# An attention and two-MLP kernel on one core: whole tiles of 64-bit words, eight heads a group, copies of q and v on GpSimd, plain products with the last weights

## The chip, the cores and the metric

One core of a Trainium2 chip runs the whole kernel as one launch. The metric is the device time of that launch in microseconds. TensorE (PE) multiplies, VectorE (DVE), ScalarE (ACT) and GpSimd (POOL) do the elementwise work, and all transfers of the kernel are issued from SyncE's queue (SP). Each engine takes its instructions in the order in which the program put them; an instruction that waits holds up everything behind it on its engine.

## The reference, cut to what matters

```python
def _attn_ref(q, k, v, g_q, g_k):            # 4 batches, 12 heads, 448 tokens, head size 64
    def rmsnorm(x, g):
        return x / np.sqrt(np.mean(x * x, axis=-1, keepdims=True) + 1e-06) * g
    q_n, k_n = rmsnorm(q, g_q), rmsnorm(k, g_k)
    scores = (1 / np.sqrt(64)) * np.matmul(q_n, k_n.transpose(0, 1, 3, 2))
    attn = np.exp(scores - np.max(scores, axis=-1, keepdims=True))
    attn = attn / (np.sum(attn, axis=-1, keepdims=True) + 1e-09)
    return np.matmul(attn, v)
# heads side by side: x is 1792 x 768
h = x @ w_in;  x = np.maximum(0.01 * h, h) @ w_out             # 768 -> 2048 -> 768
out = (((x @ w1) * (x @ w2)) @ w3) @ w_last                     # 768 -> 1024 -> 1024 -> 768
```

q, k and v are float32. The five weight matrices are float64, and the kernel gets them as pairs of 32-bit words.

## The kernel before, in words

**Arithmetic.** A product of float32 matrices is made of three float32r products: each operand is split into a high and a low part (a copy to float32r on ScalarE, then a subtraction of the copy from the operand), and TensorE multiplies high by high, high by low and low by high. The helper `copy` (L100 to L106) is a copy on ScalarE ("A"), VectorE ("V") or GpSimd ("P"), and `subtract` (L190 to L192) is the subtraction, on GpSimd or VectorE; so all of them stand in the profile at L102, L106 and L192, and are told apart by their tiles.

**Attention.** There are 48 heads and 50 steps. In step s, `attention_steps` (L392) emits the values of head s-2, the four transposes of the softmax of head s-1, the four score tiles of head s, and then the preparations: `keys(s+5)`, `load_v(s)`, `v_split(s)`, `prep(s+2)`, `load(s+3)` and `statistics(s+6)`. A score tile goes from TensorE (L272, L273) to VectorE, which scales it and takes the extreme of each row (L276), to ScalarE for the exponential (L285). Its transposes (L316) go to ScalarE (the high part, tile pth) and then VectorE (the low part, tile ptl), and then TensorE multiplies them with v (L370). `prep` splits q: the copy qh on ScalarE, the subtraction ql on GpSimd. `v_split` splits v of heads 8 to 47 in the same way.

`statistics(i)` (L127) does nothing but for the heads i that begin a group in `GROUPS` (L38): two heads at 0 and at 2, then four heads at 4, 8 and so on to 44. For a group it loads q and k of each head, squares them on ScalarE (L140) and sums them on VectorE (L141); then VectorE makes 1 / rms of all of the group's heads at once, by a shift and three Newton steps on a tile of 112x32 (`inverse_root`, L114 to L125; group 0 takes a power on GpSimd instead). The part for k is written to DRAM and read back spread over the partitions in `keys` (rk_sb, L238), for two heads at a time; there VectorE multiplies k by it (L239).

**MLP work between the steps.** The weights' own product w3 @ w_last is made first (`combine_weights`, tile wc), and then the two MLPs for batches 0 and 1. `fill` (L1024) spreads their matmuls between the attention steps in proportion to the steps done. After every third matmul `group` (L523) calls `pump`, which emits one more piece of weight preparation as long as fewer than two prepared tiles are waiting (`AHEAD`).

**64-bit words.** `Weights.work` (L494) prepares a weight tile of 128x768 or 128x512 in four pieces: `split`, `to_float32` for each half, and `load`. `to_float32` (L450) works on half a tile, 384 or 256 words, with five operations: ScalarE scales the high words (L467), GpSimd keeps the sign (L468), VectorE shifts and merges (L469), ScalarE scales the low words (L472), and GpSimd adds them (L473). 80 tiles come as 64-bit words: 8 of w_last, 16 of w_in and 16 of w1 and w2 (768 words wide), 16 of w3 and 24 of w_out (512 words wide). Each is loaded in two halves.

**Last pair of batches.** When the attention is done, the MLPs of batches 2 and 3 run alone (L1077 on). The products with w_in, w1 and w2 are made from 2x2 blocks with seven products instead of eight (`quads`, L852; `Operands.put`, L801, makes the sums of the operand, `Blocks`, L700, those of the weights). The products with w_out are plain (`group`, L918). The products with wc, the last of the kernel, are made from blocks as well: `of_hidden` (L831) has tiles for seven operands, `h.put` (L939, L943) fills them, and `quads(ONE, ...)` (L962) multiplies; this happens twice, for g = 0 and 1. The low parts of the weights of the second MLP are subtracted on GpSimd (`eng`, L747), those of the first on VectorE.

**Order.** A scheduler that plays a timeline through when the program is built sets the order on each engine from readiness and priority: `PRIORITY` (L43) ranks the attention functions, and weight preparation has 100.

Of the kernel before, what the change touches and what calls it, by code (L numbers as in the profile page):

```python
# [8 lines left out]
F32 = mybir.dt.float32  # L9
# [11 lines left out]
P = 128  # L21
# [16 lines left out]
GROUPS = {0: 2, 2: 2, **{i: 4 for i in range(4, 48, 4)}}  # L38
MAX_GROUP = 4
# [9 lines left out]
def attention_then_moe(  # L49
# [22 lines left out]

# [14 lines left out]
    cv = right(name="cv", bufs=4)  # L87
# [38 lines left out]

    def statistics(i):  # L127

        n = GROUPS.get(i)
        if n is None:  # L130
            return
        m = NCH * n
        ss = small.tile([CP, 2, MAX_GROUP * NCH], F32, tag="ss", name="ss", bufs=2)[:, :, :m]
        for j in range(n):
            b, e = divmod(i + j, H)
            x = io.tile([CP, 2, NCH, D], F32, tag="qk", name="qk_sb", bufs=2)
            nc.sync.dma_start(x, qk[b, e])
            after = exps.get(i - STATS_AHEAD)
            with tc.issue_after(after.ins) if after else ExitStack():
                nc.scalar.activation(x, x, AF.Square)  # L140
            nc.vector.tensor_reduce(  # L141
                ss[:, :, j * NCH : (j + 1) * NCH], x, axis=AX.X, op=ALU.add
            )
# [107 lines left out]
    def v_split(i):  # L251
# [4 lines left out]
        copy("A", h["vs"][:, :, 0], h["v"])  # L256
# [157 lines left out]
    class Weights:  # L414
# [20 lines left out]
        def load(self, t):  # L435
# [6 lines left out]
            self.words[t] = []  # L442
            for e in range(2):
                x = cv.tile([P, WT // 2, 2], U32, tag="w64", name="w64")
                half = src[:, e * n : (e + 1) * n].rearrange("p (n t) -> p n t", t=2)
                with tc.issue_after(start["ins"].ins) if t < 2 else ExitStack():
                    nc.sync.dma_start(x[:, : n // 2], half)
                self.words[t].append(x)

        def to_float32(self, t, e):  # L450
# [8 lines left out]
            m = self.size(t) // 2  # L459
            if e == 0:  # L460
                self.raw[t] = wp.tile([P, WT], F32, tag="raw", name="raw")
            words = self.words[t][e]
            low, high = words[:, :m, 0], words[:, :m, 1]
            out = self.raw[t][:, e * m : (e + 1) * m]
# [3 lines left out]
            nc.gpsimd.tensor_scalar(signed, signed, 0.0, 1.0, op0=ALU.mult, op1=ALU.mult)  # L468
            nc.vector.scalar_tensor_tensor(  # L469
# [3 lines left out]
            nc.gpsimd.tensor_tensor(top, top, low, op=ALU.add)  # L473

        def split(self, t):
# [3 lines left out]
            self.words.pop(t, None)  # L479
# [14 lines left out]
        def work(self):  # L494
            n = len(self.sources)
            for t in range(-2, n):
# [3 lines left out]
                if 0 <= t + 1 < n and self.sources[t + 1][1]:  # L500
                    for e in range(2):
                        self.to_float32(t + 1, e)
                        yield
# [196 lines left out]
    class Blocks:  # L700
# [5 lines left out]
        def __init__(self, sources, shared):  # L706
            self.sources, self.shared = sources, shared
# [27 lines left out]
        def work(self):  # L735
            self.load(0)
            yield
            for q, of in enumerate(self.sources):
# [8 lines left out]
                eng = "P" if q >= self.shared else "V"  # L747
# [5 lines left out]
                self.split(a, ("wh", "wl"), wp, eng)  # L753
# [10 lines left out]
                self.split(f[1], ("wh", "wl"), wp, eng)  # L764
# [26 lines left out]
    class Operands:  # L791
# [9 lines left out]
        def put(self, k, what, x):  # L801
# [3 lines left out]
            if what != "12":  # L805
                two(x, t[{"11": 1, "21": 2, "22": 3}[what]], k, "V")
            sub = nc.vector.tensor_tensor
            if "t2" not in f and all(n in f for n in ("11", "12", "22")):
                f["t1"], f["t3"], f["t2"] = f["11"], f["12"], f["22"]
# [5 lines left out]
                two(f["t1"], t[5], k, "V")  # L815
            if "t4" not in f and "t2" in f and "21" in f:
# [14 lines left out]
    def of_hidden():  # L831
        return Operands(
            {
                p: [
                    [
                        last["pool"].tile([P, S], F32R, tag=f"g{part}", name=f"g{part}", bufs=14)
                        for _ in range(KG // 2)
                    ]
                    for part in "hl"
                ]  # L840
                for p in range(1, 8)
            }
        )

    ONE = [(0, x) for x in "b1 c7 b6 a2 b5 c4 b3".split()]
    TWO = [
# [5 lines left out]
    def quads(order, qs, xs, use):  # L852

        banks = {}
        for i, (bank, p) in order:
# [28 lines left out]
    def first_of_last():  # L884

        q = 0
        for g in range(NG):
# [3 lines left out]
            def use(i, p, ps):  # L891
# [6 lines left out]
                else:  # L898
                    return
                x = tuple(  # L900
                    last["pool"].tile([P, S], F32R, tag=f"g{part}", name=f"g{part}", bufs=14)
                    for part in "hl"
                )
                copy("A", x[0], y[i, what])
                subtract("V", x[1], y[i, what], x[0])
                gs[int(what[1]) + 1][2 * i + int(what[0]) - 1] = x

            yield from quads(TWO, [q, q + 1], last["x"], use)
            q += 2
            if g == NG - 1:  # L910
                last["x2"] = of_features()
            for m in range(NO):
                w = blocks.weights(q)
                w = [[x[:, k // 2, k % 2] for k in range(KG)] for x in w]
                q += 1
                for b in (3, 2):
                    ps = last["ps"].tile([P, 512], F32, tag="st", name="ps_o")
                    yield from group(blocks, ps, S, w, [gs[b][k] for k in range(KG)])  # L918
                    if g == 0:
                        acc_last(m, b)  # L920
                        nc.scalar.activation(acc[m, b], ps[:, :S], AF.Copy)
                    else:
                        nc.vector.tensor_tensor(acc[m, b], ps[:, :S], acc[m, b], op=ALU.add)
                    if g == NG - 1:
                        last["x2"].put(m // 2, f"{m % 2 + 1}{b - 1}", acc[m, b])
        last["q"] = q

    def second_of_last():
        q, x = last["q"], last["x2"]
        for g in range(2):  # L930
            h = of_hidden()
            for k in range(KH2 // 2):
                y = {}

                def use(i, p, ps):
                    if partial(y, i, p, ps) and p == 4:
                        a = y[i, "11"]
                        nc.vector.tensor_tensor(a, a, y[i, "21"], op=ALU.mult)
                        h.put(k, "21" if i else "11", a)  # L939
                    elif p == 3:  # L940
                        b = y[i, "22"]
                        nc.vector.tensor_tensor(b, ps, b, op=ALU.mult)  # L942
                        h.put(k, "22" if i else "12", b)  # L943

                yield from quads(TWO, [q, q + 1], x, use)
                q += 2
            for n in range(NO // 2):

                def use(_, p, ps):
                    what = SUMS[p]  # L950
                    m, b = 2 * n + int(what[0]) - 1, int(what[1]) + 1
                    if p in (1, 7, 6, 3) and g == 0:
                        acc_last(m, b)
                        nc.scalar.activation(acc[m, b], ps, AF.Copy)
                    else:
                        nc.vector.tensor_tensor(acc[m, b], ps, acc[m, b], op=ALU.add)  # L956
                    if p in (2, 5, 4, 3) and g == 1:
                        nc.sync.dma_start(
                            out_t[m * P : (m + 1) * P, b * S : (b + 1) * S], acc[m, b]
                        )  # L960

                yield from quads(ONE, [q], h, use)  # L962
                q += 1

    def last_sources():
# [6 lines left out]
        for g in range(2):  # L972
            yield from pairs(kept[second_mlp, g])
            js = slice(g * KH2, (g + 1) * KH2)
            yield from pairs([wc[m, :, js].rearrange("p k c -> p (k c)") for m in range(NO)])

    def begin_last_pair():
# [11 lines left out]
        for k in range(KD // 2):  # L989
            for what in ("11", "12", "22", "21"):  # L990
                x = last["f"].tile([P, S], F32, tag="x_f", name="x_f", bufs=4)
# [59 lines left out]
    with tc.tile_pool(name="comb", bufs=1) as pool:  # L1051
# [16 lines left out]
        blocks = Blocks(list(last_sources()), NG * (KG // 2 + NO))  # L1068
# [8 lines left out]
    for part in first_of_last, second_of_last:  # L1077
        for _ in part():
            pass
# [44 lines left out]
```

## Time and profile before

| | |
|---|---|
| median of 3 runs | 1304.16 us (1303.16 to 1304.36) |
| the profiled execution | 1303.81 us |
| its span, first to last instruction | 1302.0 us |
| busy: PE, DVE, ACT, POOL | 1182.5, 847.3, 762.2, 643.2 us |
| mean granted TensorE clock | 0.959 |

The span is what the trace shows; the profiled execution's own time has 1.8 us more, that lie around it. Busy time is the sum of the engine's instructions, and the end of a matmul is modelled, so a busy TensorE may still be slowed. An idle time in brackets names what ended it.

### The profile page before, as it was taken

To read this page: it belongs to the slowest core of one execution; us is meant where nothing else is said; L and a number is where in the kernel's file an instruction comes from. 1 tells how busy PE (TensorE), PEld (TensorE's weight loads), DVE (VectorE), ACT (ScalarE), POOL (GpSimd) and SP (SyncE) were. 2 spreads that over 40 slices of the span, in tenths; PEclk is the share of its full clock that TensorE was granted. 3 is DMA by queue.
4 is the path that set the end of the run, shared out by engine and by line. 5 is a ranking of instruction groups with operands and counts; after the bars stand their busy time and mean duration, and the time that the engine had idled before them with its cause. 6 is when DMAs were issued, how large, how long until landed. Compare 5 with 4: busy or idle time off the path is not lost. (4 is left out here: it accounts for less than half of the span.)

```text
span 1302.0 us, 18289 instructions
## 1 busy us (share of the span) xinstructions
PE 1182.5 (91%) x5780; PEld 1015.7 (78%) x5780; DVE 847.3 (65%) x1593; ACT 762.2 (59%) x1657; POOL 643.2 (49%) x657
## 2 busy tenths in 40 slices
PE   3888989988888889999888999999999999899997
PEld 2436877877777779887777898898999999697986
DVE  6777676787967586773684444448346464986576
ACT  6676777787956667665674566535443434444432
POOL 6887666888933368776787447520000000222321
PEclk9889998998989899999999999999999999998999
DMA  8677666677674456574355245125112120211212
GB/s 240 166 177 212 180 165 190 197 201 193 191 200 146 126 151 181 166 206 140 115 167 183 85 115 175 55 92 191 54 45 81 33 82 25 84 46 46 72 46 85
DMA packets 108577, 172.66 MB, mean 133 GB/s; under 512 B 23776, under 2 KB 62656, under 8 KB 108480
## 3 DMA queue, kind: packets, MB, share of 16 engines
q1 hardware_dynamic: 108480, 171.50, 45.8%
q8 instruction: 45, 0.74, 0.2%
q14 instruction: 52, 0.43, 0.1%
HBM read 130.45 MB, written 30.45 MB: 124 GB/s over the span
## 5 line engine op out<-in xcount | busy, mean ns | idle before, releaser
L192 POOL TENSOR_TENSOR wl<-raw,wh 128x512 fp32r<-128x512 f32 (+1 forms) x97 | 156.1, 1609 | 321.7 <-ACT wh L730 252.8
L473 POOL TENSOR_TENSOR raw<-raw,w 128x384 uint32<-128x384 uint32 (+1 forms) x160 | 155.9, 981 | 39.2 <-DVE raw L469 31.1
L285 ACT ACTIVATE p<-p,low 112x448 f32<-112x448 f32 x192 | 126.9, 662 | 71.4 <-DVE p L276 71.0
L469 DVE SCALAR_TENSOR_TENSOR raw<-raw,w 128x384 uint32<-128x384 uint32 (+1 forms) x160 | 126.3, 803 | 60.0 <-POOL w L468 56.1
L316 PE MATMUL pt<-ident,p 112*112 112x112 f32 x768 | 119.2, 278 | 48.5 <-DVE ptl L192 33.9
L316 PEld LDWEIGHTS pt<-ident,p 112*112 112x112 f32 x768 | 89.2, 141 | 88.9 <-DVE ptl L192 39.1
L276 DVE TENSOR_SCALAR_CACHE_REDUCE p<-ps,rs 112x448 f32<-112x448 f32 x192 | 125.1, 676 | 40.7 <-PE ps L273 24.1
L192 DVE TENSOR_TENSOR ptl<-pt,pth 112x448 fp32r<-112x448 f32 x160 | 97.0, 616 | 79.3 <-ACT pth L102 77.9
L531 PE MATMUL ps_mm<-xh,wl 128*128 128x448 f32 x384 | 143.6, 375 | 1.2 <-POOL wl L192 1.2
L531 PE MATMUL ps_mm<-xh,wh 128*128 128x448 f32 x384 | 143.7, 375 | 0.8 <-ACT wh L489 0.8
L531 PE MATMUL ps_mm<-xl,wh 128*128 128x448 f32 x384 | 143.2, 373 | 0.0
L472 ACT ACTIVATE w<-w 128x384 uint32<-128x384 uint32 (+1 forms) x160 | 78.4, 491 | 96.5 <-DMA w<-w 41.2
L531 PE MATMUL ps_mm<-gh,wl 128*128 128x448 f32 x288 | 106.8, 374 | 1.2 <-DVE wl L192 1.0
L272 PE MATMUL ps<-ks,qh 128*112 128x448 f32 x192 | 79.9, 419 | 30.9 <-DVE p L276 22.4
L531 PE MATMUL ps_mm<-gl,wh 128*128 128x448 f32 x288 | 107.8, 376 | 0.0
L531 PE MATMUL ps_mm<-gh,wh 128*128 128x448 f32 x288 | 107.4, 377 | 0.2
L468 POOL TENSOR_SCALAR w<-w 128x384 f32<-128x384 f32 (+1 forms) x160 | 82.4, 527 | 39.6 <-ACT raw L467 34.5
L102 ACT ACTIVATE pth<-pt 112x448 fp32r<-112x448 f32 (+1 forms) x176 | 92.1, 532 | 16.0 <-PE pt L316 12.2
L467 ACT ACTIVATE raw<-w 128x384 f32<-128x384 f32 (+1 forms) x160 | 74.0, 487 | 39.9 <-DMA w<-w3t 9.4
L489 ACT ACTIVATE wh<-raw 128x512 fp32r<-128x512 f32 (+1 forms) x104 | 73.1, 704 | 17.4 <-PE ps_mm L531 13.0
L531 PEld LDWEIGHTS ps_mm<-xh,wh 128*128 128x128 f32 x384 | 73.7, 192 | 7.7 <-ACT wh L489 1.4
L531 PEld LDWEIGHTS ps_mm<-xh,wl 128*128 128x128 f32 x384 | 73.6, 192 | 7.6 <-POOL wl L192 1.4
(172 smaller groups left out, 3115.6 us busy)
## 6 DMA issues: line engine op xcount, KB each, us to landing
w<-w_in SPq DMA_DIRECT2D x32, 384.0 KB, 4.8
w<-w_out SPq DMA_DIRECT2D x48, 256.0 KB, 3.6
w<-w SPq DMA_DIRECT2D x32, 384.0 KB, 4.5
qk_sb<-qk SPq DMA_DIRECT2D x48, 224.0 KB, 4.0
qt_sb<-qt SPq DMA_DIRECT2D x96, 112.0 KB, 3.3
raw<-kept_first_mlp SPq DMA_DIRECT2D x24, 384.0 KB, 3.8
raw<-kept_first_mlp SPq DMA_DIRECT2D x36, 256.0 KB, 2.7
w<-w3t SPq DMA_DIRECT2D x32, 256.0 KB, 3.7
```

Source lines behind the costliest of these rows:

```text
L102: nc.scalar.activation(out, x, AF.Copy)
L192: e.tensor_tensor(out, x, y.bitcast(F32), op=ALU.subtract)
L272: nc.tensor.matmul(ps, h["qh"][:, q], h["ks"], start=True, stop=False)
L276: nc.vector.tensor_scalar(p, ps, h["scale"][:, c : c + 1], None, op0=ALU.mult, op1=ALU.min, accum_out=low,)
L285: exps[i] = nc.scalar.activation(p, p, AF.Exp, bias=low, scale=-1.0, accum_out=h["sum"][:, c : c + 1])
L316: nc.tensor.transpose(pt[:, c * CP : (c + 1) * CP], h["p"][c][:, kc * CP : (kc + 1) * CP], ident[:CP, :CP],)
L467: nc.scalar.activation(out, signed, AF.Copy, scale=2.0**-112)
L468: nc.gpsimd.tensor_scalar(signed, signed, 0.0, 1.0, op0=ALU.mult, op1=ALU.mult)
L469: nc.vector.scalar_tensor_tensor(top, top, 3, high, op0=ALU.logical_shift_left, op1=ALU.bitwise_or)
L472: nc.scalar.activation(low, low, AF.Copy, scale=2.0**-29)
L473: nc.gpsimd.tensor_tensor(top, top, low, op=ALU.add)
L531: nc.tensor.matmul(ps[:, :n], a, x, start=begin, stop=end, skip_group_check=on)
```

## The change

- `GROUPS` has eight heads a group from head 8 on. The squares and sums of a group's heads are emitted one head a step (`squares`), the last of them in the step that makes 1 / rms.
- The copies of q in `prep` and of v in `v_split` go from ScalarE to GpSimd.
- `to_float32` works on a whole tile, so each of its operations is emitted once a tile; the add of the low words goes from GpSimd to VectorE; its five operations are three pieces for `pump`. A tile is loaded at once, into one of two buffers of twice the size.
- Products with wc are plain: `quads(ONE, ...)` and `of_hidden` go, and `output_last`, which has the loops that the products with w_out had, serves both MLPs. Blocks remain for w_in, w1 and w2.
- The low parts of all block weights are subtracted on VectorE. In `Operands.put` the split of "22" comes after those of the sums, and t2 has a tile of its own.

```diff
-GROUPS = {0: 2, 2: 2, **{i: 4 for i in range(4, 48, 4)}}
+GROUPS = {0: 2, 2: 2, 4: 4, **{i: 8 for i in range(8, 48, 8)}}
...
+    def squares(i, h):
+        first = max(g for g in GROUPS if g <= h)
...
+        nc.sync.dma_start(x, qk[b, e])
...
+            nc.scalar.activation(x, x, AF.Square)
+        nc.vector.tensor_reduce(
+            sums[first][:, :, j * NCH : (j + 1) * NCH], x, axis=AX.X, op=ALU.add
+        )
...
     def statistics(i):
+        for g, m in GROUPS.items():
+            for j in range(m):
+                if i == (g if g < 8 else max(STATS_AHEAD, g - m + 1 + j)):
+                    squares(i, g + j)
         n = GROUPS.get(i)
...
-        copy("A", h["qh"], h["qt"])
+        copy("P", h["qh"], h["qt"])
...
-        copy("A", h["vs"][:, :, 0], h["v"])
+        copy("P", h["vs"][:, :, 0], h["v"])
...
-        def to_float32(self, t, e):
+        def to_float32(self, t):
...
             nc.scalar.activation(out, signed, AF.Copy, scale=2.0**-112)
             nc.gpsimd.tensor_scalar(signed, signed, 0.0, 1.0, op0=ALU.mult, op1=ALU.mult)
+            yield
             nc.vector.scalar_tensor_tensor(
                 top, top, 3, high, op0=ALU.logical_shift_left, op1=ALU.bitwise_or
             )
             nc.scalar.activation(low, low, AF.Copy, scale=2.0**-29)
-            nc.gpsimd.tensor_tensor(top, top, low, op=ALU.add)
+            yield
+            nc.vector.tensor_tensor(top, top, low, op=ALU.add)
+            yield
...
-                self.split(a, ("wh", "wl"), wp, eng)
+                self.split(a, ("wh", "wl"), wp, "V")
...
-                self.split(f[1], ("wh", "wl"), wp, eng)
+                self.split(f[1], ("wh", "wl"), wp, "V")
...
+    def output_last(q, gs, begin, done):
+        for m in range(NO):
+            w = blocks.weights(q + m)
+            w = [[x[:, k // 2, k % 2] for k in range(KG)] for x in w]
+            for b in (3, 2):
+                ps = last["ps"].tile([P, 512], F32, tag="st", name="ps_o")
+                yield from group(blocks, ps, S, w, [gs[b][k] for k in range(KG)])
...
-            h = of_hidden()
-            for k in range(KH2 // 2):
+            gs = {b: {} for b in (2, 3)}
+            for k in range(0, KH2, 2):
...
-                        h.put(k, "21" if i else "11", a)
+                        hidden_last(a, gs, 2, k + i)
...
-                yield from quads(ONE, [q], h, use)
...
+            yield from output_last(q, gs, g == 0, store if g else None)
```

`hidden_last` makes one high and one low part of a hidden tile: a copy on ScalarE and a subtraction on VectorE.

## Rows read from the trace of the kernel before

**Rows 1.** Stages (us): length, busy PE, PEld, DVE, ACT, POOL (count), PEclk, DMA.
```profile
20.00:850.00 830.00, 744.56 (x3698) 621.88 (x3697) 553.13 (x1102) 563.56 (x1309) 572.32 (x606) 0.94 0.58 164
850.00:1106.00 256.00, 254.53 (x1244) 232.82 (x1243) 137.74 (x226) 107.97 (x192) 9.41 (x7) 1.00 0.25 75
1106.00:1182.00 76.00, 70.19 (x330) 62.04 (x329) 66.81 (x109) 34.60 (x60) 20.69 (x9) 0.98 0.19 60
1182.00:1195.00 13.00, 10.51 (x34) 7.71 (x33) 9.24 (x15) 6.43 (x12) 2.54 (x2) 0.74 0.11 32
1195.00:1268.00 73.00, 73.00 (x356) 66.51 (x355) 47.99 (x81) 31.23 (x54) 20.52 (x12) 1.00 0.20 63
1268.00:1277.00 9.00, 6.06 (x20) 4.06 (x20) 6.97 (x11) 3.99 (x8) 1.36 (x2) 0.81 0.00 0
```

**Rows 2.** TensorE's waits, 20 to 850 us: total us, times, longest us.
```profile
PE pt L316 <- DVE ptl L192: 33.9, 25, 5.0
PE ps L272 <- DVE p L276: 22.4, 18, 4.6
```

**Rows 3.** Timeline of TensorE at two places: start, duration, idle time before.
```profile
434.74 0.71 PE L272 MATMUL ps<-ks,qh 128*112 128x448 f32 x1 [4.64 <-DVE p L276]
...
487.40 0.99 PE L316 MATMUL pt<-ident,p 112*112 112x112 f32 x4 [4.56 <-DVE ptl L192]
```

**Rows 4.** Timeline of VectorE at three places.
```profile
432.52 0.69 DVE L239 SCALAR_TENSOR_TENSOR kt_sb<-kt_sb,gqk,rk_sb 128x448 f32<-128x448 f32 x1 [7.92 <-DMA rk_sb<-rk]
...
482.81 1.74 DVE L123 SCALAR_TENSOR_TENSOR rt<-ss,rs 112x32 f32<-112x32 f32 x1
...
654.78 4.33 DVE L469 SCALAR_TENSOR_TENSOR raw<-raw,w 128x384 uint32<-128x384 uint32 x1
```

**Rows 5.** Timeline of GpSimd at the third of these places.
```profile
654.67 1.84 POOL L192 TENSOR_TENSOR wl<-raw,wh 128x768 fp32r<-128x768 f32 x1
656.48 2.23 POOL L192 TENSOR_TENSOR xl<-acc,xh 128x448 fp32r<-128x448 f32 x2
```

**Rows 6.** Sums of stages: 18 us from nine inverse roots; the stretches between.
```profile
sum 162.00, PE 128.98 PEld 107.66 DVE 114.94 ACT 95.18 POOL 99.62; mean PE 14.33 PEld 11.96 DVE 12.77 ACT 10.58 POOL 11.07
...
sum 486.00, PE 447.95 PEld 391.75 DVE 324.58 ACT 341.94 POOL 343.04; mean PE 49.77 PEld 43.53 DVE 36.06 ACT 37.99 POOL 38.12
```

**Rows 7.** Lines by form, VectorE, 20 to 850 us (mean ns).
```profile
L469 DVE SCALAR_TENSOR_TENSOR raw<-raw,w 128x384 uint32<-128x384 uint32 x78 | 64.1, 837 | 30.2 <-POOL w L468 26.4 <-DMA w<-w 3.7
L469 DVE SCALAR_TENSOR_TENSOR raw<-raw,w 128x256 uint32<-128x256 uint32 x80 | 60.4, 767 | 28.7 <-POOL w L468 28.5
...
L239 DVE SCALAR_TENSOR_TENSOR kt_sb<-kt_sb,gqk,rk_sb 128x448 f32<-128x448 f32 x23 | 25.3, 1101 | 57.6 <-DMA rk_sb<-rk 31.1 <-DMA kt_sb<-kt 9.0 <-issue 8.8
...
L116 DVE TENSOR_SCALAR rs<-ss 112x32 uint32<-112x32 uint32 x11 | 17.3, 1576 | 0.1
...
L192 DVE TENSOR_TENSOR wl<-raw,wh 128x512 fp32r<-128x512 f32 x12 | 14.6, 1224 | 7.4 <-ACT wh L489 7.4
...
L192 DVE TENSOR_TENSOR wl<-raw,wh 128x768 fp32r<-128x768 f32 x5 | 4.8, 952 | 1.2 <-ACT wh L489 1.2
```

**Rows 8.** Stage, VectorE, instructions on tile rt (L123 to L125).
```profile
20.00:850.00 830.00, 36.70 (x99) 0.94 0.58 164
```

**Rows 9.** The page's costliest groups: the adds of the low bits.
```profile
L473 POOL TENSOR_TENSOR raw<-raw,w 128x384 uint32<-128x384 uint32 (+1 forms) x160 | 155.9, 981 | 39.2 <-DVE raw L469 31.1
```

**Rows 10.** Lines by form, whole span, ScalarE and GpSimd.
```profile
L467 ACT ACTIVATE raw<-w 128x384 f32<-128x384 f32 x80 | 41.2, 547 | 19.4 <-DMA w<-w_last 8.3 <-DMA w<-w_in 6.0 <-POOL wl L192 4.7
...
L467 ACT ACTIVATE raw<-w 128x256 f32<-128x256 f32 x80 | 32.8, 427 | 20.5 <-DMA w<-w3t 9.4 <-DMA w<-w_out 8.5 <-POOL wl L192 1.6
...
L102 ACT ACTIVATE qh<-qt_sb 128x448 fp32r<-128x448 f32 x48 | 27.3, 568 | 1.7 <-DMA qt_sb<-qt 1.0 <-PE ps L272 0.6
...
L102 ACT ACTIVATE vs<-v_sb 112x256 fp32r<-112x256 f32 x40 | 16.4, 411 | 0.4
...
L106 POOL TENSOR_SCALAR kh<-kt_sb 128x448 fp32r<-128x448 f32 x23 | 14.6, 637 | 33.1 <-DVE kt_sb L239 33.1
```

More of the change, by code (lines that the diff above doesn't have):

```diff
@@ L125, in inverse_root @@
             nc.vector.scalar_tensor_tensor(r, t, 1.5, r, op0=ALU.add, op1=ALU.mult)
+    sums = {}
+    def squares(i, h):
+        first = max(g for g in GROUPS if g <= h)
+        if first not in sums:
+            sums[first] = small.tile([CP, 2, MAX_GROUP * NCH], F32, tag="ss", name="ss", bufs=2)
+        j = h - first
+        b, e = divmod(h, H)
+        x = io.tile([CP, 2, NCH, D], F32, tag="qk", name="qk_sb", bufs=2)
+        nc.sync.dma_start(x, qk[b, e])
+        after = exps.get(i - STATS_AHEAD)
+        with tc.issue_after(after.ins) if after else ExitStack():
+            nc.scalar.activation(x, x, AF.Square)
+        nc.vector.tensor_reduce(
+            sums[first][:, :, j * NCH : (j + 1) * NCH], x, axis=AX.X, op=ALU.add
+        )
     def statistics(i):
+        for g, m in GROUPS.items():
+            for j in range(m):
+                if i == (g if g < 8 else max(STATS_AHEAD, g - m + 1 + j)):
+                    squares(i, g + j)
         n = GROUPS.get(i)
@@ L132, in statistics @@
         m = NCH * n
[L133 to L143, printed above, removed]
+        ss = sums.pop(i)[:, :, :m]
         nc.vector.tensor_scalar(ss, ss, 1.0 / D, 1e-6, op0=ALU.mult, op1=ALU.add)
@@ L441, in load @@
                 return
[L442 to L448, printed above, removed]
-        def to_float32(self, t, e):
[L459 to L462, printed above, removed]
+            x = self.words[t] = cv.tile([P, WT, 2], U32, tag="w64", name="w64")
+            with tc.issue_after(start["ins"].ins) if t < 2 else ExitStack():
+                nc.sync.dma_start(x[:, :n], src.rearrange("p (n t) -> p n t", t=2))
+        def to_float32(self, t):
+            m = self.size(t)
+            self.raw[t] = wp.tile([P, WT], F32, tag="raw", name="raw")
+            words = self.words.pop(t)
             low, high = words[:, :m, 0], words[:, :m, 1]
-            out = self.raw[t][:, e * m : (e + 1) * m]
+            out = self.raw[t][:, :m]
             top = out.bitcast(U32)
@@ L500, in work @@
                 if 0 <= t + 1 < n and self.sources[t + 1][1]:
-                    for e in range(2):
-                        self.to_float32(t + 1, e)
-                        yield
+                    yield from self.to_float32(t + 1)
                 if t + 2 < n:
@@ L804, in put @@
             f[what] = x
-            if what != "12":
-                two(x, t[{"11": 1, "21": 2, "22": 3}[what]], k, "V")
+            if what in ("11", "21"):
+                two(x, t[{"11": 1, "21": 2}[what]], k, "V")
             sub = nc.vector.tensor_tensor
             if "t2" not in f and all(n in f for n in ("11", "12", "22")):
-                f["t1"], f["t3"], f["t2"] = f["11"], f["12"], f["22"]
+                f["t1"], f["t3"] = f["11"], f["12"]
+                f["t2"] = last["f"].tile([P, S], F32, tag="x_f", name="t2", bufs=5)
                 sub(f["t1"], f["12"], f["11"], op=ALU.subtract)
@@ L829, in of_features @@
         return Operands(tiles)
[L831 to L846, printed above, removed]
+    ORDER = [
         (int(x[0]), x[1:])
@@ L882, in acc_last, with hidden_last, last_pair @@
         acc[m, b] = last["f"].tile([P, S], F32, tag=name, name="acc", bufs=1)
-    def first_of_last():
+    def hidden_last(x, gs, b, k):
+        gs[b][k] = tuple(
+            last["pool"].tile([P, S], F32R, tag=f"g{part}", name=f"g{part}", bufs=8)
+            for part in "hl"
+        )
+        copy("A", gs[b][k][0], x)
+        subtract("V", gs[b][k][1], x, gs[b][k][0])
+    def output_last(q, gs, begin, done):
[5 more added lines that the diff above has]
+                yield from group(blocks, ps, S, w, [gs[b][k] for k in range(KG)])
+                if begin:
+                    acc_last(m, b)
+                    nc.scalar.activation(acc[m, b], ps[:, :S], AF.Copy)
+                else:
+                    nc.vector.tensor_tensor(acc[m, b], ps[:, :S], acc[m, b], op=ALU.add)
+                if done:
+                    done(m, b, acc[m, b])
+    def last_pair():
         q = 0
+        x2 = None
         for g in range(NG):
@@ L899, in use, with done @@
                     return
[L900 to L908, printed above, removed]
+                hidden_last(y[i, what], gs, int(what[1]) + 1, 2 * i + int(what[0]) - 1)
+            yield from quads([q, q + 1], last["x"], use)
             q += 2
+            done = None
             if g == NG - 1:
[L911 to L929, printed above, removed]
+                x2 = of_features()
+                def done(m, b, x):
+                    x2.put(m // 2, f"{m % 2 + 1}{b - 1}", x)
+            yield from output_last(q, gs, g == 0, done)
+            q += NO
         for g in range(2):
-            h = of_hidden()
-            for k in range(KH2 // 2):
+            gs = {b: {} for b in (2, 3)}
+            for k in range(0, KH2, 2):
                 y = {}
@@ L942, in use, with store @@
                         nc.vector.tensor_tensor(b, ps, b, op=ALU.mult)
-                        h.put(k, "22" if i else "12", b)
-                yield from quads(TWO, [q, q + 1], x, use)
+                        hidden_last(b, gs, 3, k + i)
+                yield from quads([q, q + 1], x2, use)
                 q += 2
[L947 to L960, printed above, removed]
-                yield from quads(ONE, [q], h, use)
-                q += 1
+            def store(m, b, x):
+                nc.sync.dma_start(out_t[m * P : (m + 1) * P, b * S : (b + 1) * S], x)
+            yield from output_last(q, gs, g == 0, store if g else None)
+            q += NO
     def last_sources():
@@ L974, in last_sources @@
             js = slice(g * KH2, (g + 1) * KH2)
-            yield from pairs([wc[m, :, js].rearrange("p k c -> p (k c)") for m in range(NO)])
+            yield from ([wc[m, :, js].rearrange("p k c -> p (k c)")] for m in range(NO))
     def begin_last_pair():
```

24 lines of the change are left out of this document (11 added, 13 removed).

## The prediction, made before the change was run

> **What bounds the kernel now.** I read the busy time by stage first [rows 1]. From 850 us on, in the last pair of batches, TensorE is the bound: 254.5 of 256 us busy at full clock in the first stretch, and in 1195 to 1268 us 356 matmuls take 73 us, which is 0.205 us each. Two holes break this, at 1182 and 1268 us. Before 850 us no engine is full: TensorE 745 of 830 us, VectorE 553, ScalarE 564, GpSimd 572. TensorE stands for 85 us there, and its mean granted clock is 0.94. Of its two levels, 1.2 and 2.4 GHz, that mean means 12% of the time at the lower, so some 50 us of work lost on top. This stage is a ring of queues in order, and the question is which wait ends last.
>
> The second view, TensorE's waits in that stage, says that: it waits for VectorE, 33.9 us for the low part of the transposed softmax (psum is freed by that subtraction) and 22.4 us for the scaled scores [rows 2]. Third, I went to the longest of these waits in the timeline. TensorE stood 4.64 us until 434.74 and 4.56 us until 487.40 [rows 3]. In the first, VectorE had been idle 7.92 us: the multiplication of k waited for 1 / rms to come back from DRAM, with the scores behind it in the queue. In the second, it was in the small operations of `inverse_root`, one of which took 1.74 us for 32 elements a partition [rows 4]. Both are events of a group of four heads. A third place is of another kind: one merge of 64-bit words took 4.33 us [rows 4] where the mean is 0.84 [rows 7], while GpSimd ran three subtractions without a gap [rows 5].
>
> To see what the group events weigh altogether I summed nine stretches of 18 us, each from the start of an inverse root, and the nine stretches between them [rows 6]. TensorE is busy 129.0 of 162 us (79.6%) in the first and 448.0 of 486 (92.2%) in the others. The 12.6% are 20.4 us, 2.3 us a group.
>
> **The change, part by part.**
>
> *Groups of eight.* From 13 groups it comes to 8: the five that began at 12, 20, 28, 36 and 44 go. At 2.3 us each that is 11.5 us. The five groups of eight have one head's loads, squares and sum in their step instead of four; so 1 / rms is ready earlier and the first keys of a group wait less. L239 stands idle 57.6 us in all [rows 7]. I take half of 2.3 us for each of these five, 6 us, between 0 (the trip to DRAM remains) and 11.5. The squares themselves are moved, not saved: six heads' loads, squares and sums now come in step 0, hidden by nothing, for the start is full; I leave that at up to 3 us, in the range. Sum: -17.5 us, between -8 and -23. The five roots also free VectorE: L116 at 1.576 us [rows 7], and 36.70 us of Newton steps over 11 groups, 3.34 us each [rows 8]; 4.9 us a group, 25 us in all, though they are counted within the 2.3 us already where TensorE felt them.
>
> *Whole tiles.* The 160 half-tile passes become 80.
> - ScalarE: 547 ns for 384 words against 427 for 256 [rows 10] leaves 187 ns that don't depend on the length; 160 fewer operations save 30 us.
> - VectorE's merge: 837 and 767 ns for 384 and 256 words [rows 7], 70 ns per 128 words. For 768 that gives 1.05 us, for 512 0.91, so 40 of each cost 78 us instead of 125: -46 us; at worst nothing is saved.
> - VectorE's new add: the trace has none. Its nearest rows are VectorE's subtractions from two SBUF tiles in this stage, 0.952 us for 768 and 1.224 for 512 columns [rows 7]; 40 of each are 87 us. Against uncontended work it could be some 70, and if each waits as long as the merges do it is 100.
> - GpSimd loses 155.9 us of adds [rows 9].
>
> *Copies of q and v.* ScalarE gives up 27.3 + 16.4 us. GpSimd's copy of k, 637 ns for 448 columns, is the nearest row [rows 10]: 48 of them are 31 us, and the 40 of v, with 256 columns, at most 25. GpSimd's own subtraction behind each copy no longer waits for ScalarE.
>
> Together in this stage: ScalarE -74 us of 564, GpSimd -100 of 572, VectorE +87 - 46 - 25 = +16 of 553. Only VectorE is what TensorE waits for. Sixteen us more of it, 3%, would cost TensorE between 0 (they fall where it waits anyway) and 16 us (each in front of a score). Against that, VectorE waited 55 us for GpSimd at the merges (the two idle times of L469 [rows 7]), behind a GpSimd that now has less to do and sends its part one `pump` earlier; if half of this goes and TensorE felt a third, that is 9 us. I take the two as equal: 0, between -25 and +25. In it are also the pieces of `pump`, five a tile instead of four, where a product with w_out for one batch gives only four chances, and the first operation of a tile that now waits for the whole load. Two prepared tiles in hand, and a freer ScalarE, hide both; without that cover it is the +25.
>
> A rule speaks against this part. Here one merge was held 4.33 us while three GpSimd operations passed [rows 4, 5]. The Trainium skill, "SBUF — State Buffer", section "Who interferes with whom", says that a VectorE instruction with two SBUF inputs contends with a GpSimd instruction that reads SBUF, and that the one which comes first keeps the shared port for its whole length. By that rule all 80 adds join the 80 merges in that contest, while GpSimd's own adds leave it; the trace agrees on who waits, but here the wait was longer than any one of the three instructions. What that could cost is the slower rival below.
>
> *The last pair.* Plain products with wc are 2 x 144 matmuls where blocks took 2 x 126: 36 more, 7.4 us at 0.205. What goes are the holes: the first output of each g needed sums of sums of the last hidden tile, and TensorE did 34 matmuls (7.0 us) in 13 us and 20 (4.1 us) in 9 [rows 1]: 6.0 + 4.9 = 10.9 us lost. In the plain form the last hidden tile needs one copy and one subtraction, and the matmuls that don't need it (the other three hidden tiles, and for the second batch twelve more) go first, 9 to 21 matmuls or 1.8 to 4.3 us of cover. Without that cover the holes stay and it is +7.4. VectorE takes 16 low parts of weights from GpSimd, 15 us at 0.952 [rows 7], which would matter around 1106 to 1182 us, where it is busy 66.8 of 76 us [rows 1]; but 28 operations for sums and parts of hidden tiles leave it, though none of them before 1130 us, so I allow +3 there. Sum: -3.5 us, between -7 and +10.
>
> **Sum**: 1303.8 (the profiled execution's own time; span 1302.0) - 17.5 + 0 - 3.5 = 1282.8. The median of the runs is 0.35 us above that execution: 1283.2.
>
> **Rivals.**
> - *More falls than the groups.* If VectorE, with shorter waits for both other engines, is late half as often everywhere, half of its 56.3 us [rows 2] goes, and with it the clock's loss in proportion (50 us lost per 85 us of standing): 28 x 1.6 = 45 us, then -3.5: 1255. For it: ScalarE and GpSimd fall by 13 and 17%. Against: VectorE's own load does not fall.
> - *VectorE held by GpSimd.* The slower one. GpSimd's copy and subtraction of q now run without a gap, as the three at 654.67 us did [rows 5], and every merge and add behind such a run waits. If the 160 VectorE operations wait 0.6 us more each, that is 96 us, and with the 16 above VectorE's load goes from 67 to 80%. A third of this in front of TensorE is +37, less 17.5 and 3.5: 1320. It decides from about 0.35 us more a wait (56 + 16 us, a third of which, 24, eats the 21). For it: the 4.33 us; that 512 columns took 1.224 us and 768 only 0.952 [rows 7], so waits of that order are there. Against: GpSimd is busy 69% now and 57% then.
> - *Given back.* The groups' 17.5 us are eaten by VectorE's 16 and its order: 1304 less 3.5, within about 1300 to 1306.
> - *The groups don't do it.* The round trip stays as late in each group that is left and only the five that go count, with squares crowded at the start: 1303.8 - 11.5 + 3 - 3.5 = 1292.
>
> **How the numbers follow.** Forecast (1265 to 1298) 0.48, more falls 0.15, groups don't do it 0.07, given back 0.10, VectorE held 0.20. About 0.2%, 2.6 us, is what a measurement of this kernel tells from no change. Faster takes the first three, with 0.02 of "given back": 0.72, less 0.02 for the forecast's own tail; "given back" leaves 0.07 within and a little above. So 0.70, 0.07, 0.23. The range leaves out half of the two outer cases: 1250 to 1315.
>
> **What would show it.** In the profile after: seven inverse roots instead of twelve, and TensorE's busy share after them near 90%; idle time of L239 about 20 us instead of 57.6; VectorE's merge near 1.0 us and its add below 1.2; TensorE's waits for VectorE about 40 us and a mean clock of 0.95 or more before 850 us; the last pair starting some 15 to 20 us earlier; no hole of several us in front of the products with wc. The prediction is wrong if merges or adds average over 1.4 us, if TensorE waits for weights, or if VectorE's waits for ScalarE's high part take the place of those removed.

## The result, and the profile after

The changed kernel takes 1286.5 us (median of 4 runs, 1284.3 to 1293.6) against 1304.1 before: a ratio of 0.9888, 95% interval 0.9857 to 0.9919. Measured again beside the variants below, on another chip on which the kernel before takes 1297.7, the ratio is 0.9918 (0.9892 to 0.9944). So the change is worth 1.0%, some 11 to 18 us; 1283.2 was forecast. The profiled execution took 1287.95 us, with a span of 1286.2.

The view of the stages, for the changed kernel, with the columns of [rows 1]:

```profile
20.00:852.00 832.00, 749.18 (x3764) 631.86 (x3765) 571.85 (x1044) 519.76 (x1073) 492.17 (x460) 0.96 0.56 165
...
1140.00:1286.00 146.00, 141.84 (x691) 129.25 (x689) 71.19 (x116) 46.05 (x80) 0.00 (x0) 1.00 0.19 63
```

The first row is to be held against the first of [rows 1]: in about the same time TensorE does 66 matmuls more (3764 to 3698). GpSimd is 80 us less busy, ScalarE 44 us less and VectorE 19 us more, where the sum had -100, -74 and +16 (busy time counts instructions that overlap at their ends once, and durations were summed). TensorE still stands for 83 us. The load of x for the last pair is issued at 852.3 us instead of 865.3, and from there to the end it is 433.9 us instead of 436.7.

TensorE's waits in that stage, as in [rows 2]:

```profile
PE pt L327 <- DVE ptl L203: 25.8, 17, 5.3
PE ps L283 <- DVE p L287: 16.4, 12, 4.5
PE pt L327 <- ACT pth L101: 4.3, 2, 2.5
```

The two waits for VectorE fall from 56.3 to 42.2 us. But over all rows of the view the sum falls only from 84.2 to 82.6: waits for ScalarE and GpSimd come up in their place (17.9 to 29.1 us). The rest of the stage's gain is in TensorE's busy time: the mean granted clock is 0.96 instead of 0.94. A second profile of the changed kernel has 0.95 there, so how much of that the change brings can't be told from it.

VectorE by line and form, 20 to 838 us, against [rows 7]:

```profile
L476 DVE SCALAR_TENSOR_TENSOR raw<-raw,w 128x768 uint32<-128x768 uint32 x39 | 49.1, 1262 | 37.1 <-POOL w L474 37.1
L481 DVE CUSTOM_DVE_ANT_0 raw<-w,raw 128x1536 uint16<-128x1536 uint16 x39 | 45.6, 1169 | 0.6
L476 DVE SCALAR_TENSOR_TENSOR raw<-raw,w 128x512 uint32<-128x512 uint32 x40 | 37.7, 943 | 37.0 <-POOL w L474 36.9
L481 DVE CUSTOM_DVE_ANT_0 raw<-w,raw 128x1024 uint16<-128x1024 uint16 x40 | 36.2, 906 | 1.3 <-ACT pth L101 0.5
...
L250 DVE SCALAR_TENSOR_TENSOR kt_sb<-kt_sb,gqk,rk_sb 128x448 f32<-128x448 f32 x23 | 25.8, 1124 | 33.8 <-DMA kt_sb<-kt 6.6 <-issue 6.4 <-DMA v_sb<-v 6.2
```

Merges cost 87 us where 78 were put, adds 82 where 87 were put. The multiplication of k stands idle 33.8 us instead of 57.6, and of that the wait for 1 / rms to come back from DRAM is 5.0 us instead of 31.1:

```profile
DVE kt_sb L250 <- DMA rk_sb<-rk: 5.0, 2, 2.8
```

The wait of the merges for GpSimd's part did not fall, as was hoped, but rose from 55 to 74 us.

Of the stretches of 18 us from an inverse root on, four are left after 100 us, against nine in [rows 6]:

```profile
sum 72.00, PE 58.57 PEld 52.10 DVE 58.42 ACT 39.88 POOL 40.00; mean PE 14.64 PEld 13.03 DVE 14.61 ACT 9.97 POOL 10.00
```

TensorE is busy 81% there (58.6 of 72), much as it was (79.6%). By this an event of eight heads is not seen to be cheaper than one of four, though the four stretches range from 71 to 92%; there are fewer of them.

The chain of waits at the end, in order of time, has the two products with wc:

```profile
1176.53 23.71 PE ps_o L537 x117
...
1260.39 22.27 PE ps_o L537 x108
```

They run at 0.203 and 0.206 us a matmul, and in place of the holes at 1182 and 1268 us in [rows 1] TensorE waits once, for 0.8 us.

### The profile page after: what moved, and what is told of

It reads as the page before. It is cut to its first block, busy times and chain, and to the rows that moved or that the text cites. A ratio compares the mean times of both kernels' runs of the same rounds, so it can differ in the third digit from the quotient of the medians.

```text
span 1286.2 us, 17311 instructions
## 1 busy us (share of the span) xinstructions
PE 1177.4 (92%) x5816; PEld 1019.6 (79%) x5816; DVE 827.8 (64%) x1474; ACT 700.3 (54%) x1385; POOL 505.6 (39%) x477
## 4 chain that ended last, share of the span: by engine, by line
PE 54%; DMA 14%; DVE 11%; issue 8%; POOL 8%; ACT 3%; SPq 2%; POOLq 0%; DVEq 0%; ACTq 0%
PE ps_mm L537 15%; PE ps_o L537 12%; PE ps_b L537 9%; PE ps_c L537 5%; DMA w<-w_out 3%; PE pt L327 2%; PE pw L537 2%; PE ps_a L537 2%; PE po L381 2%; DVE raw L476 2%; POOL wl L203 2%; DMA ks<-kt_sb 2%; DVE raw L481 2%; DMA kt_sb<-kt 1%; DMA w<-w_in 1%
## 5 line engine op out<-in xcount | busy, mean ns | idle before, releaser
L203 POOL TENSOR_TENSOR wl<-raw,wh 128x512 fp32r<-128x512 f32 (+1 forms) x83 | 133.5, 1609 | 99.5 <-ACT wh L497 99.5
L327 PE MATMUL pt<-ident,p 112*112 112x112 f32 x768 | 115.1, 271 | 37.4 <-DVE ptl L203 25.8
L203 DVE TENSOR_TENSOR ptl<-pt,pth 112x448 fp32r<-112x448 f32 x160 | 97.0, 618 | 76.8 <-ACT pth L101 72.5
L476 DVE SCALAR_TENSOR_TENSOR raw<-raw,w 128x768 uint32<-128x768 uint32 (+1 forms) x80 | 87.8, 1099 | 75.6 <-POOL w L474 75.5
L101 ACT ACTIVATE pth<-pt 112x448 fp32r<-112x448 f32 (+1 forms) x176 | 92.1, 535 | 42.8 <-PE pt L327 32.7
L479 ACT ACTIVATE w<-w 128x768 uint32<-128x768 uint32 (+1 forms) x80 | 63.2, 790 | 82.9 <-DMA w<-w_out 26.0
L537 PE MATMUL ps_o<-gl,wh 128*128 128x448 f32 x288 | 104.9, 365 | 0.0
L537 PE MATMUL ps_o<-gh,wl 128*128 128x448 f32 x288 | 102.5, 365 | 0.0
L283 PE MATMUL ps<-ks,qh 128*112 128x448 f32 x192 | 79.2, 416 | 24.7 <-DVE p L287 16.4
L537 PE MATMUL ps_o<-gh,wh 128*128 128x448 f32 x288 | 99.2, 365 | 0.8 <-DVE s L943 0.8
L474 POOL TENSOR_SCALAR w<-w 128x768 f32<-128x768 f32 (+1 forms) x80 | 66.8, 835 | 74.2 <-ACT raw L473 65.5
L473 ACT ACTIVATE raw<-w 128x768 f32<-128x768 f32 (+1 forms) x80 | 62.8, 785 | 60.4 <-DMA w<-w3t 16.4
```

The source lines that it names most:

```text
L101: nc.scalar.activation(out, x, AF.Copy)
L203: e.tensor_tensor(out, x, y.bitcast(F32), op=ALU.subtract)
L283: nc.tensor.matmul(ps, h["qh"][:, q], h["ks"], start=True, stop=False)
L327: nc.tensor.transpose(pt[:, c * CP : (c + 1) * CP], h["p"][c][:, kc * CP : (kc + 1) * CP], ident[:CP, :CP],)
L473: nc.scalar.activation(out, signed, AF.Copy, scale=2.0**-112)
L476: nc.vector.scalar_tensor_tensor(top, top, 3, high, op0=ALU.logical_shift_left, op1=ALU.bitwise_or)
```

## The experiments: one part alone

All ran for five rounds beside the kernel before on their chip. First, each of the four parts of the change alone in the kernel before.

**Groups alone** (`GROUPS`, `MAX_GROUP`, `squares`, `statistics`).

```diff
-GROUPS = {0: 2, 2: 2, **{i: 4 for i in range(4, 48, 4)}}
-MAX_GROUP = 4
+GROUPS = {0: 2, 2: 2, 4: 4, **{i: 8 for i in range(8, 48, 8)}}
+MAX_GROUP = 8
```

Expected: 

> The kernel before with groups of eight heads and squares spread over the steps, nothing else. Theory of the prediction (the events of a group cost TensorE 2.3 us each, and the five that remain of eight heads get cheaper): 17 us faster than before, between 8 and 23; VectorE's wait for rk_sb, 31 us before, under 10. Rival (the gain of the whole change comes from the engines that it relieves, by the words and the copies): less than 5 us.

Measured: ratio 0.9899 (0.9870 to 0.9928), which is 13 us. VectorE's waits in this kernel, 20 to 850 us, have for the way through DRAM:

```profile
DVE kt_sb L251 <- DMA rk_sb<-rk: 13.4, 5, 4.1
```

Five waits instead of the seven that made 31.1 us in [rows 7]. The groups' gain is there without any of the rest; the wait is above the 10 us that were set. TensorE's two waits for VectorE fall from 56.3 us [rows 2] to 42.8:

```profile
PE ps L284 <- DVE p L288: 26.0, 20, 4.2
PE pt L328 <- DVE ptl L204: 16.8, 20, 3.2
```

**Words alone** (`load`, `to_float32`, `work`, the two buffers).

```diff
-            nc.gpsimd.tensor_tensor(top, top, low, op=ALU.add)
+            yield
+            nc.vector.tensor_tensor(top, top, low, op=ALU.add)
```

Expected: 

> The kernel before with whole tiles of 64-bit words and the add on VectorE, nothing else. Theory of the prediction (VectorE gains 41 us of work, 87 of adds less 46 in the merges, without the 25 us that the groups save; GpSimd and ScalarE lose 156 and 30): no clear change, within 8 us of before. Rival (relieving GpSimd and ScalarE is the gain): 8 us or more faster. Rival (VectorE is held by GpSimd at the 160 operations): 8 us or more slower.

Measured: 1.0023 (0.9995 to 1.0051), 3 us slower or nothing. GpSimd falls by 143 us on the page (643.2 to 499.8), ScalarE by 15 (30 were put), and nothing is gained by it; VectorE goes up by 46 (847.3 to 893.3).

**Copies alone.**

```diff
-        copy("A", h["qh"], h["qt"])
+        copy("P", h["qh"], h["qt"])
...
-        copy("A", h["vs"][:, :, 0], h["v"])
+        copy("P", h["vs"][:, :, 0], h["v"])
```

Expected: 

> The kernel before with the copies of q and v on GpSimd, nothing else. Theory of the prediction (ScalarE loses 44 us, GpSimd gains up to 56, and neither is what TensorE waits for): within 4 us of before. Rival (GpSimd's copy and subtraction without a gap hold VectorE's merges): 4 us or more slower, with the merges over 0.9 us on average instead of 0.8.

Measured: 1.0242 (1.0213 to 1.0272), 31 us slower. TensorE's waits and VectorE's merges in this kernel:

```profile
PE pt L316 <- DVE ptl L192: 43.3, 26, 5.0
PE ps L272 <- DVE p L276: 35.9, 19, 5.2
```

```profile
L469 DVE SCALAR_TENSOR_TENSOR raw<-raw,w 128x384 uint32<-128x384 uint32 x77 | 76.8, 1013 | 20.3 <-POOL w L468 20.1
L469 DVE SCALAR_TENSOR_TENSOR raw<-raw,w 128x256 uint32<-128x256 uint32 x80 | 67.9, 864 | 20.8 <-POOL w L468 20.7
```

The theory fell: 52 us more on GpSimd and 32 less on ScalarE cost 31 us. GpSimd is busy for 52% of the span here, but nearly all of it lies before 850 us, where it was busy for 69% already in the kernel before. The signs that the rival named are there. The merges take 1013 and 864 ns instead of 837 and 767, and TensorE waits 79.2 us for VectorE in the two rows instead of 56.3. VectorE's wait for GpSimd's part before the merges falls (40.8 us instead of 54.9), so that wait is not the cost. With the 1.6 of the prediction (clock lost along with standing) the 22.9 us that TensorE waits more are 37.

**Plain products alone** (`output_last`, `hidden_last`, the operands, the block weights on VectorE).

```diff
-                yield from quads(ONE, [q], h, use)
+            yield from output_last(q, gs, g == 0, store if g else None)
```

Expected: 

> The kernel before with plain products with wc (36 matmuls more) and all block weights subtracted on VectorE, nothing else. Theory of the prediction: 3.5 us faster (7.4 us of matmuls added, 10.9 us of holes gone), between 7 faster and 3 slower. Rival (the holes only change their place): 7 us slower.

Measured: 0.9974 (0.9952 to 0.9995), 3.4 us faster. Its attention stage is, instruction for instruction on TensorE, that of the kernel before, and yet in its profile the last pair begins at 857.1 instead of 865.3 us: two profiles of the same order differ by 8 us here (they are of two chips, on which the kernel before takes 1304 and 1298 us), so smaller differences are read here from the timed rounds alone.

Alone the parts sum to -13 + 3 + 31 - 3 = +18 us. The whole is -11 to -18. So they don't add up.

## The experiments: all but one part

These leave one of the same four edits out of the changed kernel.

Without the words: 

> The changed kernel with half tiles and the add on GpSimd as before: groups, copies and plain products without the words. If the parts add up as measured alone (groups -13, copies +32, plain -3): 15 us slower than before, about 1313 to 1318. Theory (copies cost because GpSimd, full with the adds, holds VectorE's merges): the same or a little better, 5 to 20 us slower, with merges over 0.9 us. Rival (the copies' loss came from the groups' events, which are fewer now): no slower than before.

Measured: 1.0061 (1.0037 to 1.0085), 7 us slower than before, merges at 1030 and 869 ns. Against the whole (0.990, between its two measurements) the words are worth 1.6% here, and alone they were worth nothing.

Without the copies: 

> The changed kernel with the copies of q and v on ScalarE as before: groups, words and plain products. If the parts add up: -13 + 3 - 3 = 13 us faster than before, so that the copies cost nothing in the whole change. Theory (copies cost by way of a full GpSimd, and the words empty it): within 4 us of the changed kernel. Rival (the copies cost 30 us wherever they stand): 30 us faster than the changed kernel. Rival (with room on GpSimd the copies are a gain, because ScalarE is relieved): 5 us or more slower than the changed kernel.

Measured: 0.9831 (0.9809 to 0.9854), 1271.75 us: the fastest of all, faster than both kernels. The copies cost about 0.7%, 9 us, in the whole, more than the 4 that were set, and 31 alone. With groups of four they cost nothing that can be seen beside the words: words alone and plain products alone multiply to 0.9997, and the kernel that has the copies as well, the next one, has 0.9964. Why they cost something with groups of eight is not shown.

Without the groups: 

> The changed kernel with groups of four heads as before: words, copies and plain products. Theory (the groups' gain of 13 to 17 us does not depend on the rest): 13 to 17 us slower than the changed kernel, about the time of before. Rival (part of the gain in the changed kernel comes from words and copies together): at least 6 us faster than before.

Measured: 0.9964 (0.9943 to 0.9985). The groups are worth 0.6% in the whole, some 8 us, where 13 to 17 were expected, and 1.0% alone; the intervals of these two overlap. Words, copies and plain products together make the other 4 or 5 us.

Without the plain products: 

> The changed kernel with blocks for wc as before: groups, words and copies. Theory (the last pair runs by itself and its 3 us do not depend on the rest): 3 us slower than the changed kernel, between 0 and 7.

Measured: 0.9999 (0.9974 to 1.0023), 1.0% above the whole where 0.3% was expected. In its profile the holes are back:

```profile
PE ps_c L538 <- ACT gh L102: 4.8, 2, 2.4
```

and the last pair takes 439.1 us instead of 433.9. That is 5 of the 13; where the others come from stays open, as its runs spread from 1288.6 to 1303.4.

## The experiments: what the copies and the groups cost

**The add back on GpSimd**, in the changed kernel.

```diff
-            nc.vector.tensor_tensor(top, top, low, op=ALU.add)
+            nc.gpsimd.tensor_tensor(top, top, low, op=ALU.add)
```

Expected: 

> The changed kernel with the add of the low words back on GpSimd, whole tiles as in the change. Theory (the words help the copies by taking the adds off GpSimd): 10 to 20 us slower than the changed kernel, with merges well over the 1.26 and 0.94 us that they take there. Rival (whole tiles alone, fewer and longer operations, make the room): within 5 us of the changed kernel. Rival (VectorE is what counts, and it is rid of 83 us of adds): 5 us or more faster.

**The changed kernel again**, on the same chip. Expected: 

> The changed kernel itself, beside the variants on their chip. If the parts measured one by one added up (groups -13, words +3, copies +32, plain -3) it would be 19 us slower than before; it was measured 1.1% faster, and theory says that it stays so, 11 to 17 us faster than before: the words and the copies don't add up, since the words empty GpSimd, on which the copies lean.

Measured: 1.0018 (0.9992 to 1.0044) for the first and 0.9918 for the second, 13 us apart. The merges with the add on GpSimd:

```profile
L476 DVE SCALAR_TENSOR_TENSOR raw<-raw,w 128x768 uint32<-128x768 uint32 x39 | 61.7, 1584 | 37.7 <-POOL w L474 37.7
L476 DVE SCALAR_TENSOR_TENSOR raw<-raw,w 128x512 uint32<-128x512 uint32 x40 | 43.5, 1086 | 27.6 <-POOL w L474 27.5
```

They grow from 1262 and 943 ns, though VectorE has 45 us less to do on the page (827.8 to 783.2). So not the length of the tiles made most of the room but the add that left GpSimd. Four kernels share the groups and the plain products, and differ in where copies and adds run and, the last, in the length of the tiles:

| groups of eight, plain products, and | GpSimd busy, us | median, us |
|---|---|---|
| words, no copies | 451.1 | 1271.75 |
| words and copies (the change) | 505.6 | 1286.5 and 1286.9 |
| words with the add on GpSimd, and copies | 613.3 | 1301.1 |
| copies, no words | 635.9 | 1303.5 |

In these four the time goes with GpSimd's load: 185 us more of it from the first to the last, on an engine that is busy for less than half of the span in each, and 32 us more time. But the load by itself does not set the time: the groups alone, with GpSimd busy 645.2 us, take 1285.2 us, and the words alone, with 499.8, take 1301.0. What the load does to VectorE is another question (below).

**A third buffer for the parts of q and v**, in the changed kernel.

```diff
-        h["qh"] = att.tile([P, S], F32R, tag="qh", name="qh", bufs=2)
+        h["qh"] = att.tile([P, S], F32R, tag="qh", name="qh", bufs=3)
...
-        h["vs"] = att.tile([CP, NCH, 2, D], F32R, tag="vs", name="vs")
+        h["vs"] = att.tile([CP, NCH, 2, D], F32R, tag="vs", name="vs", bufs=3)
```

Expected: 

> The changed kernel with a third buffer for the parts of q (qh, ql) and of v (vs); one buffer instead of two for the sums of squares makes the room. It takes away the waits of GpSimd's copies for TensorE to release a buffer (58 us in the changed kernel, 31 at vs and 27 at qh), with the words' sign behind them in GpSimd's queue. Theory (what the copies cost in the changed kernel, some 7 us, is that queue): 4 to 10 us faster than the changed kernel, VectorE's waits for GpSimd at the merges well under 74 us. Rival (the cost is GpSimd holding VectorE's operations from two SBUF tiles): no change.

Measured: 0.9937 (0.9914 to 0.9960), no better than the changed kernel. GpSimd's and VectorE's waits, 20 to 850 us:

```profile
POOL vs L105 <- PE po L381: 34.3, 14, 6.6
```

```profile
DVE raw L476 <- POOL w L474: 42.7, 25, 4.6
```

The wait at v did not go (31.3 us before the edit), so the edit is no full test of it. VectorE's wait for GpSimd at the merges did fall, from 74 to 43 us, but the merges themselves grew, from 1262 and 943 ns to 1368 and 1138; so the run does not tell what that queue costs by itself.

**Groups of four, with the squares spread over the steps**, in the kernel before.

```diff
-GROUPS = {0: 2, 2: 2, 4: 4, **{i: 8 for i in range(8, 48, 8)}}
-MAX_GROUP = 8
+GROUPS = {0: 2, 2: 2, **{i: 4 for i in range(4, 48, 4)}}
+MAX_GROUP = 4
```

(against the kernel with the groups alone). Expected: 

> The kernel before with the squares of a group spread over the steps, but groups of four as before. It parts the groups' 13 us into the number of groups and the spreading. Theory of the prediction (11.5 of 17.5 us by the number, 6 by the earlier 1 / rms): 3 to 6 us faster than before. Rival (the late 1 / rms, with VectorE's queue behind it, is all of it): 10 to 13 us faster, as eight heads a group were. Rival (the number is all): no change.

Measured: 1.0056 (1.0033 to 1.0080), 7 us slower than before. VectorE's waits:

```profile
DVE kt_sb L251 <- DMA rk_sb<-rk: 35.7, 10, 6.0
```

Spreading alone gives nothing back at the multiplication of k (31.1 us in the kernel before, and 38.5 with the plain products alone, whose order in this stage is the same) and costs 7 us; the cause of that loss is not shown. The kernel with the groups alone differs from this one by the number and the size of the groups only, and that is 1.0056 - 0.9899 = 1.6%, 20 us.

## Why the prediction was right, and where its steps were not

**Groups.** -17.5 us was put, -13 measured alone, and in the whole some -8. Both terms were mis-sized. The number of groups made 20 us, if the whole difference between the two kernels with spread squares is put down to the five events that go: 4 us each where 2.3 were read from the busy shares in [rows 6], which hold only what falls within 18 us. The other term was 6 us of gain, since "1 / rms is ready earlier and the first keys of a group wait less". The keys do wait less with eight heads (13.4 us, and 5.0 in the whole), but spreading the squares was a loss of 7 us with groups of four. That the two errors nearly cancel is luck.

The trace of the kernel before also shows what makes an inverse root dear, which the prediction read as the price of its small operations. The operation of 1.74 us [rows 4] began 0.11 us after GpSimd had begun a subtraction that took 1.80. A little later, while GpSimd stood idle for 3.17 us, the same operation took 0.18:

```profile
482.70 1.80 POOL L192 TENSOR_TENSOR wl<-raw,wh 128x768 fp32r<-128x768 f32 x1
...
489.93 1.02 POOL L473 TENSOR_TENSOR raw<-raw,w 128x384 uint32<-128x384 uint32 x1 [3.17 <-DVE raw L469]
```

```profile
487.87 0.18 DVE L123 SCALAR_TENSOR_TENSOR rt<-ss,rs 112x32 f32<-112x32 f32 x1
```

Of the 66 instructions of this form that write rt, 40 had no GpSimd instruction beside them and took at most 0.19 us; the other 26 took 0.65 us on average. All 121 instructions of this form in the inverse roots took 57.8 us; at 0.19 us each they would be 23. So the groups' events and the copies act in part by one mechanism: VectorE is held while GpSimd works.

**Whole tiles and copies.** Zero was put for the two together, and the whole leaves little else for them. But it is not that each costs nothing: the copies alone cost 31 us, and the words give that back; that these two cancel was not foreseen either. The step that failed is "only VectorE is what TensorE waits for", from which a load on GpSimd was taken as free. The sizes of the operations were right (adds 82 us for 87, merges 87 for 78).

**The slower rival** had the mechanism, VectorE held by GpSimd, and a point from which it decides: 0.35 us more a wait. With the copies alone the merges took only 0.18 and 0.10 us more and the time rose by 31 us; with the add on GpSimd 0.32 and 0.14 us, and 13 us. By the Trainium skill's rule ("SBUF — State Buffer", "Who interferes with whom") GpSimd's operations hold such merges, and the longer merges beside a fuller GpSimd agree with it in both pairs of kernels. The rival counted merges and adds alone, but other operations of VectorE are held too. The table has an estimate of all of it from the traces, 20 to 850 us: what VectorE's instructions beside a GpSimd instruction took, beyond the median of the same operation and form with none beside it (0.06 us at most; for the few forms without such a case, beyond their shortest tenth).

| kernel | VectorE held, us | ratio |
|---|---|---|
| before | 123 | 1 |
| groups alone | 106 | 0.9899 |
| words alone | 118 | 1.0023 |
| copies alone | 151 | 1.0242 |
| plain products alone | 120 | 0.9974 |
| groups of four, squares spread | 131 | 1.0056 |
| the change, two profiles | 90 and 92 | 0.9888 and 0.9918 |
| without the words | 137 | 1.0061 |
| without the copies | 90 | 0.9831 |
| without the groups | 114 | 0.9964 |
| without the plain products | 90 | 0.9999 |
| add back on GpSimd | 105 | 1.0018 |
| third buffer | 109 | 0.9937 |

In the kernel before, the 312 instructions with none beside them differ from their medians by less than 1 us in all; the 789 others make the 123. The copies alone add 28 us of holding and 31 us of time, and the groups alone take off 17 and 13. So the cost of the copies alone fits this holding, and TensorE's 22.9 us more of waiting for VectorE there say the same. It is not all: with and without the copies the change has the same 90 us (and merges of 1294 and 980 ns without them), and yet it is faster by 0.7% without; and the words alone take off 5 us and gain nothing. By which way GpSimd's work reaches TensorE in the whole is not settled.

**The last pair.** -3.5 us was put; -3.4 was measured alone, and the holes went as described.

**What the profile was to show.** Seven inverse roots, TensorE's waits for VectorE near 40 us (42.2), the clock at 0.96 and the missing holes came. TensorE's share after an inverse root stayed at 81%, L250's idle time at 33.8 us where 20 were named, and the last pair starts 13 us earlier, not 15 to 20. The waits that took a part of the gain back were not those that had been named: VectorE's wait for ScalarE's high part, the danger that was set down, fell from 77.9 to 72.5 us, and it is TensorE's own waits for ScalarE that rose (16.5 to 24.2 us).

## What to carry to other kernels

An engine that is idle for half of the span can be busy in the stage that counts (GpSimd 69% before 850 us), and its work can lengthen another engine's instructions: look for an instruction that takes several times its usual time, see what ran beside it, and measure the move alone, since here it was hidden behind another edit that emptied the engine. Where a small serial piece of work stalls the queue of the engine that is waited for, make it rarer, not only earlier. And when a change has several parts, leave each out once: the version without the copies is 1.7% faster than the kernel before and some 0.7% faster than the changed one.

## What the runs showed of the hardware

A merge from two SBUF tiles on VectorE took 4.33 us beside three GpSimd operations in a row [rows 4, 5]; another of the same form, at 681.57 us of the same trace, took 0.55. Of the 80 merges of this form in that trace, the 16 with at most 0.06 us of GpSimd's work beside them took 0.56 us at most; the other 64 took 0.91 on average. The add of 32-bit words on VectorE appears in the trace as one operation on twice as many 16-bit numbers and takes 1.17 us for 768 words, where GpSimd took 1.91 us for the same add (in the kernel with the add back on GpSimd). The Trainium skill, "VectorE: DVE Perf Modes", section "Specifications", says that integer operands are converted to float32 and exact only below 2^24; the 16-bit form fits that, but no run here tests it.
